# Weight conversion off GpSimd, even steps, and a shorter lag between front sequences, in an attention kernel followed by a low-rank mixer

## The chip, the cores and the metric

The kernel runs on one core of one Trainium2 chip. The metric is device time in microseconds (us). Runs of different sets were on different chips, so every kernel has runs of the kernel before beside it on its own chip, and ratios are taken only within such a set.

## The reference

Linear attention with decay, over blocks of 64, then a mixer of low rank over the sequence and a two-layer network. In short (4 batches, 8 heads, 768 positions, head width 64; rank 32; 512 channels; 2048 hidden):

```python
# attention, for each block of 64 positions and each head
intra = ((qb @ kb.T) * Dmask) @ vb
inter = (qb * lam_pow) @ kv_state
kv_state = lam_block * kv_state + (kb * rev_pow).T @ vb
# ... heads side by side give x: (4, 768, 512)
h = xt @ U @ V                      # over the sequence, rank 32
u = x + h.T
out = u + np.maximum(u @ w_ch1, 0.0) @ w_ch2
```

U, V, w_ch1 and w_ch2 are float64. The kernel reads them as pairs of 32-bit words and makes float32 of them itself; this is the "conversion" below.

## The kernel before

It has three stages: a **front** (attention, mix, and the transposes that the network needs), the **hidden** layer (`u @ w_ch1`, results stored to memory), and the **second product**. Each float32 product is done as three matmuls of rounded parts, which is why `u` and the weights exist as high part, low part and difference.

The conversion of one tile of 128x512, in steps that are called one at a time between other work:

```python
def one():
    hi = st["w"][:, :, 1]
    ...
    nc.vector.tensor_scalar(sc, hi, 20, 0x7FF, ALU.logical_shift_right, ALU.bitwise_and)      # L110
    nc.gpsimd.tensor_scalar(sc_f, sc, 1151.0, 896.0, ALU.min, ALU.max)                        # L111
    nc.gpsimd.tensor_scalar(sc, sc_f, -896.0, float(1 << 23), ALU.add, ALU.mult)              # L112
    nc.vector.tensor_scalar(m, hi, 0xFFFFF, 0x100000, ALU.bitwise_and, ALU.bitwise_or)        # L113

def two():
    ...
    nc.vector.scalar_tensor_tensor(m_f, lo, 2.0**-32, m, ALU.mult, ALU.add)                   # L121
    nc.vector.scalar_tensor_tensor(sc, hi, 0x80000000, sc, ALU.bitwise_and, ALU.bitwise_or)   # L122
    nc.vector.scalar_tensor_tensor(dst(), m_f, 2.0**-20, sc_f, ALU.mult, ALU.mult)            # L123

def three():                                   # the three parts of a weight tile
    nc.vector.tensor_scalar(t.bitcast(U32), w.bitcast(U32), HI, None, ALU.bitwise_and)        # L139
    nc.scalar.copy(o[:, 0, :], t)
    nc.gpsimd.tensor_tensor(out=low, in0=w, in1=t, op=ALU.subtract)                           # L141
    nc.scalar.mul(o[:, 1, :], low, 4096.0)
    nc.vector.scalar_tensor_tensor(o[:, 2, :], t, -E, low, ALU.mult, ALU.add)                 # L143
```

The front is four batches, each a list of 38 small "pieces" (transpose q and k, scores, outputs, transpose back; then two pieces `low` and `low_sum` for the mixer, then mix and turn). Batches 0 and 2 form sequence one, batches 1 and 3 sequence two, of 76 pieces each; the two are interleaved with a lag, and after every second piece one conversion step is called:

```python
one = front(0) + front(2)
two = front(1) + front(3)
lag = 3 * NT                                   # 18 pieces
merged = one[:lag]
for i in range(lag, len(one)):
    merged += [one[i], two[i - lag]]
merged += two[len(one) - lag :]
...
side = U's steps + v_steps(0) + v_steps(1) + w1_steps(0) + w1_steps(1)    # (shortened)
for i, (what, s) in enumerate(merged):
    run[what](s)
    if side and i % 2 == 1:
        side.pop(0)()
```

## Time and profile before

The time was 754.97 us, the median of 3 runs (751.0 to 755.06). The stages of the profiled run, of span 752.2 us, are read from the first and last matmul of each:

| stage | us |
|---|---|
| front, to the first hidden matmul | 198.0 |
| hidden layer | 279.5 |
| second product | 270.1 |
| end | 4.7 |

The groups of VectorE's conversion instructions, with shapes kept apart: busy time and mean of one in ns, then idle time before them.

```profile
L113 DVE TENSOR_SCALAR m<-words 128x512 uint32<-128x512 uint32 x32 | 31.5, 983 | 0.0
L121 DVE SCALAR_TENSOR_TENSOR m<-words,m 128x512 f32<-128x512 uint32 x32 | 30.1, 941 | 0.9
L139 DVE TENSOR_SCALAR wt<-wf 128x512 uint32<-128x512 uint32 x32 | 13.6, 426 | 1.7
```

L113 and L139 are the same kind of work at the same size, yet L113 takes over twice as long: GpSimd has often just begun its own work when L113 comes. By the timelines, 16 of the 32 took 1.49 to 1.52 us, each begun 0.1 us after GpSimd's subtract L141; of the others, 15 took 0.41 to 0.47.

Second, the chain of work that ended last, for the front (start, length, what):

```profile
24.07 10.12 DMA words<-in_moe_V_dram
...
41.78 8.75 DMA words<-in_moe_V_dram
```

Third, windows over the front up to the first `low` (its copy on ScalarE starts at 68.17 us) and from the first to the last `low` (184.63 us). The columns are the stretch, its length, then busy time and count of TensorE's matmuls, its weight loads, VectorE, ScalarE and GpSimd, then granted clock, share of DMA and GB/s:

```profile
8.00:68.17 60.17, 46.85 (x519) 40.32 (x520) 35.64 (x80) 18.03 (x33) 12.75 (x16) 0.86 0.63 146
68.17:184.63 116.46, 107.48 (x1315) 85.65 (x1313) 94.51 (x203) 52.31 (x95) 18.99 (x19) 1.00 0.56 145
```

### The profile page before, as it was taken

The numbers are of one execution on the slowest core, as the hardware profiler recorded it, in microseconds if no ns is written. First come the engines' busy times: TensorE is split into PE (matmuls) and PEld (weight loads), VectorE is DVE, ScalarE is ACT, GpSimd is POOL, SyncE is SP. The second block draws the span as 40 slices with busy tenths as digits, with TensorE's granted clock in tenths as the row PEclk, the third lists the DMA queues.
The fourth block names the chain that finished last, engine by engine and source line by source line (L and its number), as shares of the span: only waits on it lengthen the run. The fifth ranks groups of instructions, "written<-read, shape, count | busy, mean of one in ns | idle before, by whom it ended". The sixth has DMA issues, their size and how long they took to land.

```text
span 752.2 us, 11331 instructions
## 1 busy us (share of the span) xinstructions
PE 711.0 (95%) x4176; PEld 566.5 (75%) x4176; DVE 549.2 (73%) x961; ACT 234.6 (31%) x409; POOL 150.3 (20%) x150
## 2 busy tenths in 40 slices
PE   6669899997999999999999999999999999999997
PEld 5567668785668866888888888788888888888885
DVE  4567878795998988877677753567767676676764
ACT  2334444443223233232333322223223232322320
POOL 1213211110014444433333320002003030020300
PEclk9978999999799999999999999999999999999999
DMA  6664766750326657665565479995536335363531
GB/s 158 155 148 115 196 168 168 169 142 16 112 93 247 199 196 263 212 217 183 191 223 215 169 261 364 313 347 182 184 97 197 102 136 168 94 201 98 155 98 56
DMA packets 131808, 131.77 MB, mean 175 GB/s; under 512 B 81320, under 2 KB 89512, under 8 KB 131752
## 3 DMA queue, kind: packets, MB, share of 16 engines
q1 hardware_dynamic: 131752, 131.04, 55.1%
q8 instruction: 33, 0.54, 0.3%
q14 instruction: 23, 0.19, 0.1%
HBM read 80.68 MB, written 50.33 MB: 174 GB/s over the span
## 4 chain that ended last, share of the span: by engine, by line
PE 74%; DVE 14%; issue 4%; DMA 3%; POOL 3%; ACT 1%; SPq 1%; DVEq 0%; POOLq 0%; ACTq 0%
PE pz L512 17%; PE pz L607 12%; PE pz L606 12%; PE pd L608 12%; PE pd L518 9%; DMA words<-in_moe_V_dram 3%; PE px L302 2%; PE ps L280 2%; PE px L297 2%; DVE kv L328 2%; DVE r L526 1%; DVE sm L285 1%; DVE sc L122 1%; DVE ut L395 1%; DVE w L143 1%
## 5 line engine op out<-in xcount | busy, mean ns | idle before, releaser
L512 PE MATMUL pz<-u_hl,w 128*128 128x512 f32 x768 | 190.6, 398 | 1.9 <-ACT r L525 1.9
L512 PEld LDWEIGHTS pz<-u_hl,w 128*128 128x128 f32 x768 | 144.6, 189 | 38.9 <-ACT r L525 4.4
L608 PE MATMUL pd<-w_d,m 128*128 128x512 f32 x384 | 152.3, 397 | 0.0
L607 PE MATMUL pz<-w_hl,m 128*128 128x512 f32 x384 | 152.2, 396 | 0.0
L606 PE MATMUL pz<-w_hl,m 128*128 128x512 f32 x384 | 152.2, 396 | 0.0
L591 ACT ACTIVATE m<-mt 128x512 fp32r<-128x512 f32 x96 | 60.6, 632 | 192.6 <-PE pd L608 138.0
L592 DVE SCALAR_TENSOR_TENSOR m<-rm,m 128x512 fp32r<-128x512 f32 x96 | 71.4, 745 | 51.0 <-ACT m L591 50.6
L518 PE MATMUL pd<-u_d,w 128*128 128x512 f32 x384 | 100.7, 399 | 3.6 <-DVE u_d L501 2.7
L518 PEld LDWEIGHTS pd<-u_d,w 128*128 128x128 f32 x384 | 71.7, 188 | 24.4 <-DVE u_d L501 3.7
L608 PEld LDWEIGHTS pd<-w_d,m 128*128 128x128 f32 x384 | 72.3, 188 | 18.0 <-DVE r L526 0.4
L607 PEld LDWEIGHTS pz<-w_hl,m 128*128 128x128 f32 x384 | 72.3, 188 | 17.6
L606 PEld LDWEIGHTS pz<-w_hl,m 128*128 128x128 f32 x384 | 72.3, 188 | 17.6
L526 DVE SCALAR_TENSOR_TENSOR r<-pd,r 128x512 f32<-128x512 f32 x96 | 61.6, 682 | 32.1 <-ACT r L525 31.1
L628 POOL TENSOR_TENSOR o<-o,u 128x512 f32<-128x512 f32 x20 | 29.7, 1522 | 237.9 <-DVE o L626 237.9
L141 POOL TENSOR_TENSOR wl<-wf,wt 128x512 f32<-128x512 f32 x32 | 42.2, 1317 | 151.4 <-DVE wt L139 101.0
L593 DVE SCALAR_TENSOR_TENSOR m<-m 128x512 fp32r<-128x512 f32 x96 | 69.0, 720 | 0.9
L525 ACT ACTIVATE r<-pz 128x512 f32<-128x512 f32 x96 | 51.7, 592 | 56.2 <-PE pz L512 56.2
L590 DVE TENSOR_SCALAR mt<-rm 128x512 uint32<-128x512 uint32 x96 | 46.2, 481 | 29.4 <-DMA rm<-r_d 28.7
L140 ACT CAST w<-wt 128x512 fp32r<-128x512 f32 x32 | 19.9, 622 | 101.1 <-issue 63.6
L302 PE MATMUL px<-sm,vraw 128*64 128x128 f32 x384 | 40.4, 296 | 6.8 <-DVE sm L285 5.6
L261 POOL TENSOR_TENSOR ks<-kraw,rev 128x512 f32<-128x512 f32 x20 | 21.5, 1074 | 101.9 <-PE pkv L318 63.9
L297 PE MATMUL px<-qs,kv 128*64 128x128 f32 x320 | 35.9, 289 | 4.9 <-DVE kv L328 4.9
(70 smaller groups left out, 785.3 us busy)
## 6 DMA issues: line engine op xcount, KB each, us to landing
r_d<-r SPq DMA_DIRECT2D x96, 256.0 KB, 3.1
rm<-r_d SPq DMA_DIRECT2D x96, 256.0 KB, 2.7
words<-in_moe_w_ch_dram SPq DMA_DIRECT2D x32, 512.0 KB, 4.0
w_d<-w SPq DMA_DIRECT2D x16, 768.0 KB, 3.3
w_hl<-w_d SPq DMA_DIRECT2D x16, 512.0 KB, 6.0
qraw<-in_q_dram SPq DMA_DIRECT2D x24, 256.0 KB, 3.9
kraw<-in_k_dram SPq DMA_DIRECT2D x24, 256.0 KB, 3.7
vraw<-in_v_dram SPq DMA_DIRECT2D x24, 256.0 KB, 3.7
```

The costliest lines, as they stand in the source:

```text
L297: nc.tensor.matmul(out=px[rows, a, :], lhsT=kvs[b % 2][:, a, rows], rhs=qs[:, a, :], start=True, stop=False,)
L302: nc.tensor.matmul(out=px[x * D : (x + 1) * D, a, :], lhsT=vr[:, 2 * a + x, :], rhs=sm[:, x, a, :], start=(c == 0), stop=True,)
L512: nc.tensor.matmul(out=acc[g][0], lhsT=w[:, n, ct, :], rhs=uhl[g][:, n, ct, :], start=(ct == 0 and n == 0), stop=(ct == CT - 1 and n == 1),)
L518: nc.tensor.matmul(out=acc[g][1], lhsT=w[:, 2, ct, :], rhs=ud[g][:, ct, :], start=(ct == 0), stop=(ct == CT - 1),)
L525: nc.scalar.mul(r, pz, 1.0 + E)
L526: nc.vector.scalar_tensor_tensor(r, pd, 4096.0, r, ALU.mult, ALU.add)
L591: nc.scalar.activation(out=m[:, 0], in_=t, func=AF.Relu)
L592: nc.vector.scalar_tensor_tensor(m[:, 1], r, 0.0, hi, ALU.max, ALU.subtract)
L593: nc.vector.scalar_tensor_tensor(m[:, 2], hi, E, low, ALU.mult, ALU.subtract)
L606: nc.tensor.matmul(out=pz, lhsT=m[:, 0, cols], rhs=hl[:, 0], start=first, stop=False)
L607: nc.tensor.matmul(out=pz, lhsT=m[:, 1, cols], rhs=hl[:, 1], start=False, stop=end)
L608: nc.tensor.matmul(out=pd, lhsT=m[:, 2, cols], rhs=dd, start=first, stop=end)
```

## The change

Its intent: take GpSimd out of the conversion, so that it no longer slows VectorE (983 ns for L113 against 426 for L139) nor keeps it waiting (19.9 us ahead of L143, 8.7 ahead of L122); let the first two w1 tiles share the hidden units in which `u`'s differences are made, so that VectorE isn't full there; and start the second sequence sooner. Stores of `u` move one step later and q and k get a third buffer.

```diff
+    def set_ends(t):
+        nc.vector.memset(t[:, 0:1], 1151.0)
+        nc.vector.memset(t[:, 1:2], 255.0 * (1 << 23))
 ...
-            nc.gpsimd.tensor_scalar(sc_f, sc, 1151.0, 896.0, ALU.min, ALU.max)
-            nc.gpsimd.tensor_scalar(sc, sc_f, -896.0, float(1 << 23), ALU.add, ALU.mult)
             nc.vector.tensor_scalar(m, hi, 0xFFFFF, 0x100000, ...)
+            nc.scalar.activation(out=sc_f, in_=sc, func=AF.Relu, bias=ends[-1][:, 0:1], scale=-1.0)
+            nc.scalar.activation(out=sc, in_=sc_f, func=AF.Relu, bias=ends[-1][:, 1:2], scale=-float(1 << 23))
 ...
-            nc.gpsimd.tensor_tensor(out=low, in0=w, in1=t, op=ALU.subtract)
+            nc.vector.tensor_tensor(out=low, in0=w, in1=t, op=ALU.subtract)
 ... load():
-            ... bufs=4 if name == "v" else 2
+            ... bufs=4 if name == "v" else 3
 ... (zeros, rev, lamh now share one tile `small`; `pt` takes a turn in the ring of temporaries)
 ... mix():
-        nc.sync.dma_start(out=u_d[s], in_=xs[s])
 ... turn():
-        del xs[s]
+        nc.sync.dma_start(out=u_d[s], in_=xs.pop(s))
 ...
-    lag = 3 * NT
+    lag = 2 * NT
 ...
-    side += w1_steps(0) + w1_steps(1)
+    late = w1_steps(0) + w1_steps(1)
 ...
         if side and i % 2 == 1:
             side.pop(0)()
+        elif late and i > 4 * NT and i % 7 == 0:
+            late.pop(0)()
 ... hidden layer:
-    for ft in range(LAST):
-        side = w1_steps(ft + 2) + w2_steps(ft)
-        for i, pair in enumerate(pairs):
+    head = [(pair, ft) for pair in pairs for ft in (0, 1)]
+    body = [(pair, ft) for ft in range(2, LAST) for pair in pairs]
+    tail = [(pair, ft) for pair in pairs for ft in range(LAST, FT)]
 ... (the steps of a stretch are spread evenly over all of its units)
```

More of the change, by code (lines that the diff above doesn't have):

```diff
@@ L72 @@
     words_pool = [wconv]
+    ends = []
+    def set_ends(t):
+        nc.vector.memset(t[:, 0:1], 1151.0)
+        nc.vector.memset(t[:, 1:2], 255.0 * (1 << 23))
+        ends.append(t)
     u_d = [dram.tile([P, C], FP32, name=f"u_d{s}") for s in range(NS)]
@@ L110, in one @@
             nc.vector.tensor_scalar(sc, hi, 20, 0x7FF, ALU.logical_shift_right, ALU.bitwise_and)
-            nc.gpsimd.tensor_scalar(sc_f, sc, 1151.0, 896.0, ALU.min, ALU.max)
-            nc.gpsimd.tensor_scalar(sc, sc_f, -896.0, float(1 << 23), ALU.add, ALU.mult)
             nc.vector.tensor_scalar(m, hi, 0xFFFFF, 0x100000, ALU.bitwise_and, ALU.bitwise_or)
+            nc.scalar.activation(out=sc_f, in_=sc, func=AF.Relu, bias=ends[-1][:, 0:1], scale=-1.0)
+            nc.scalar.activation(
+                out=sc, in_=sc_f, func=AF.Relu, bias=ends[-1][:, 1:2], scale=-float(1 << 23)
+            )
         def two():
@@ L179, in load @@
         t = raw_pool.tile(
-            [P, H, D], FP32, tag=f"{name}raw", bufs=4 if name == "v" else 2, name=f"{name}raw"
+            [P, H, D], FP32, tag=f"{name}raw", bufs=4 if name == "v" else 3, name=f"{name}raw"
         )
@@ L193 @@
     v_hl, p_hl = vp[:, 0:S], vp[:, S : S + C]
+    set_ends(vp[:, S + C : S + C + 2].bitcast(FP32))
     ident = consts.tile([P, P], FP32, name="ident")
     gather = consts.tile([P, G, R], FP32, name="gather")
-    zeros = consts.tile([P, 1], FP32, name="zeros")
+    small = consts.tile([P, 16], FP32, name="small")
+    zeros = small[:, 0:1]
     mask = consts.tile([P, 2, HP, P], FP32, name="mask")
-    rev = consts.tile([P, 2, HP], FP32, name="rev")
-    lamh = consts.tile([P, HP], FP32, name="lamh")
+    rev = small[:, 8:16].rearrange("p (x a) -> p x a", x=2)
+    lamh = small[:, 4:8]
     powq = consts.tile([P, HP, P], FP32, name="powq")
@@ L355, in low @@
             )
-        pts[b] = att.tile([P, C], FP32, tag="pt", bufs=1, name="pt")
+        pts[b] = tmp("pt")
         nc.scalar.copy(pts[b], pp)
@@ L474 @@
             side.pop(0)()
-    for step in side:
+        elif late and i > 4 * NT and i % 7 == 0:
+            late.pop(0)()
+    for step in side + late:
         step()
@@ L490 @@
     )
+    set_ends(r_pool.tile([P, 2], FP32, tag="ends", bufs=1, name="ends"))
     def banks():
@@ L551, with run_units @@
     LAST = FT - 3
-    for ft in range(LAST):
-        side = w1_steps(ft + 2) + w2_steps(ft)
-        for i, pair in enumerate(pairs):
+    head = [(pair, ft) for pair in pairs for ft in (0, 1)]
+    body = [(pair, ft) for ft in range(2, LAST) for pair in pairs]
+    tail = [(pair, ft) for pair in pairs for ft in range(LAST, FT)]
+    def run_units(units, side, every=lambda i: None):
+        for i, (pair, ft) in enumerate(units):
             if ft == 0:
@@ L558 @@
             hidden(ft, pair)
-            for step in side[len(side) * i // len(pairs) : len(side) * (i + 1) // len(pairs)]:
+            for step in side[len(side) * i // len(units) : len(side) * (i + 1) // len(units)]:
                 step()
-    units = [(pair, ft) for pair in pairs for ft in range(LAST, FT)]
+            every(i)
+    run_units(head, w1_steps(2))
+    side = []
+    for ft in range(3, FT - 1):
+        side += w1_steps(ft) + w2_steps(ft - 3)
+    side += w2_steps(FT - 4)
+    run_units(body, side)
     side = w1_steps(FT - 1)
@@ L565 @@
     backs = list(range(FT))
-    for i, (pair, ft) in enumerate(units[:6]):
-        hidden(ft, pair)
-        for step in side[len(side) * i // 6 : len(side) * (i + 1) // 6]:
-            step()
-        if i >= 2:
-            w2_back(backs.pop(0))
+    run_units(tail[:6], side, lambda i: w2_back(backs.pop(0)) if i >= 2 else None)
     mid_ctx.close()
@@ L637, in ahead @@
             split(i + 2)
-    for i, (pair, ft) in enumerate(units[6:]):
+    for i, (pair, ft) in enumerate(tail[6:]):
         hidden(ft, pair)
```

## The prediction

> **What bounds the kernel now.** I read the slices of the page first, then windows over the stages, then the waits, and last the timelines of single engines. The slices show where TensorE is not full:
>
> ```profile
> PE   6669899997999999999999999999999999999997
> DVE  4567878795998988877677753567767676676764
> PEclk9978999999799999999999999999999999999999
> ```
>
> A slice is 18.8 us. TensorE is short in slices 0 to 2 (0 to 56 us) and slice 9 (169 to 188 us); elsewhere it looks full, but a busy PE is a modelled one, so I counted matmuls. The first hidden-layer matmul (pz of the first w1 tile) starts at 197.96 us, the first of the second product at 477.4, and the last ends near 747.5. These windows give the pace (span, then busy time and count for PE, PEld, DVE, ACT, POOL):
>
> ```profile
> 197.00:285.00 88.00, 83.62 (x345) 63.98 (x345) 80.88 (x127) 26.83 (x49) 30.05 (x31) 0.99 0.52 179
> 300.00:440.00 140.00, 140.00 (x600) 112.53 (x599) 108.67 (x168) 46.53 (x85) 50.87 (x52) 1.00 0.58 205
> 440.00:477.40 37.40, 37.40 (x161) 30.10 (x160) 14.48 (x24) 10.03 (x18) 0.29 (x1) 1.00 0.92 324
> 477.40:747.50 270.10, 270.10 (x1153) 216.71 (x1152) 187.31 (x307) 69.70 (x113) 29.75 (x20) 1.00 0.49 159
> ```
>
> In the last row 1152 matmuls take 270.1 us, 0.2345 us each without a gap. The hidden layer has 1152 too and takes 279.5 us (197.9 to 477.4), so it loses 279.5 - 270.1 = 9.4 us. At 0.2345 us, the 88 us of the first row would hold 375 matmuls; there are 345, so 7 us are lost there, and the rest before 300 us. In that stretch VectorE is 92% busy; from 440 to 477 it is 39% busy. VectorE is the bound early and has slack late. The time is thus 198 (front: attention and mix) + 279.5 + 270 + 4.7 (end), and only the first two can move.
>
> Inside the hidden stretch, VectorE does the differences u_d first and is then made slow by GpSimd:
>
> ```profile
> 200.22 6.10 DVE L501 SCALAR_TENSOR_TENSOR u_d<-u_hl 128x512 fp32r<-128x512 f32 x10
> ...
> 284.67 1.34 POOL L141 TENSOR_TENSOR wl<-wf,wt 128x512 f32<-128x512 f32 x1 [2.00 <-DVE wt L139]
> 284.77 1.52 DVE L113 TENSOR_SCALAR m<-words 128x512 uint32<-128x512 uint32 x1
> ...
> 290.54 0.42 DVE L113 TENSOR_SCALAR m<-words 128x512 uint32<-128x512 uint32 x1
> ```
>
> The same TENSOR_SCALAR takes 0.42 us alone and 1.52 us when GpSimd's subtract began just before it. The waits add two more, and one in the DMA queue:
>
> ```profile
> DVE w L143 <- POOL wl L141: 19.9, 15, 1.5
> DVE sc L122 <- POOL sc L112: 9.1, 18, 0.5
> SPq L379 <- DVE x_nat L378: 45.2, 21, 16.0
> ```
>
> In the front the chain of waits gives a stretch that is bound by latency at either end. At the far end, with one sequence alone:
>
> ```profile
> 185.27 1.13 PE L361 MATMUL pr<-pt,gather 128*128 128x512 f32 x2 [0.71 <-ACT pt L357]
> 188.00 0.83 PE L375 MATMUL pu<-vp 128*128 128x512 f32 x2 [1.60 <-DVE vp L368]
> ```
>
> and near the start VectorE, in order, stands still for V's words:
>
> ```profile
> 50.55 0.36 DVE L110 TENSOR_SCALAR sc<-words 128x384 uint32<-128x384 uint32 x1 [6.35 <-DMA words<-in_moe_V_dram]
> ```
>
> [...] 0.42 us for L113 alone, 0.68 to 0.69 us for the two-input instructions; so the subtract that moves to VectorE costs about 0.69. [...] the trace has no such form, and its Relu of 128x512 without that bias is 0.63 us. One table load is in the trace, and Relu is already used, so I count no new one.
>
> **Part 1, conversion without GpSimd.** VectorE's cost of one w tile before, from the group rows (128x512 forms): L110 0.42, L113 0.98, L121 0.94, L122 0.69, L123 0.69, L139 0.43, L143 0.75: 4.90 us, plus waits for GpSimd (19.9 + 9.1) / 32 = 0.91: 5.81. After: L113 falls to 0.42, L121 to 0.69 and L143 to 0.69, the subtract adds 0.69, the waits fall to nearly nothing: 0.42 + 0.42 + 0.69 + 0.69 + 0.69 + 0.43 + 0.69 + 0.69 = 4.72. That is 1.1 us a tile, 35 us of VectorE over 32 tiles, and GpSimd's 96 conversion instructions (42 + 31 + 24 us) go. [...] Off the path after 300 us, on it before.
>
> **Part 2, u's differences over two tiles and even steps.** From 197 to 300 us VectorE has u_d 24 x 0.61 (spacing in the timeline) = 15, r 30 x 0.61 = 18, and 12 conversions x 5.81 = 70: together 103 us in 103. It is exactly full. After, the first six units (34 us of TensorE, 5.63 each) hold the 24 u_d, 12 r and one conversion: 15 + 7 + 5 = 27 us. Then each unit holds 2 r and 25 conversions / 33 units: 1.3 + 0.76 x 4.72 = 4.9 of 5.63 us, 87%. So no backlog builds. What stays is the first unit: its eight u_d (4.9 us) start only after the last turn, while pz covers 3.75 us; TensorE lost 0.95 us there by the page's wait, and the cold clock (0.57 between 190 and 200 us) adds some. I keep 3 us of the 9.4: gain 6.5.
>
> **Part 3, shorter lag.** Each sequence has 76 pieces. With lag 18 the merged list has 18 solo, 58 pairs, 18 solo; with lag 12 it has 12, 64, 12. From the PE timeline: the second sequence's first transposes come at 43.86 us, the last paired ones near 174.2. So the first solo stretch is 8 to 44 us (36 us), the pairs take 130 us (2.25 each), the last solo stretch 24 us. After: the first twelve pieces end at 28.6 us in this trace, 64 pairs at 2.25 make 144, and the last twelve, mixes and turns alone, run from 188 to 198 today: 10 us. The chain low, pt, low_sum, vp before them (182.7 to 188) now lies beside the other sequence's last turns; I leave 2 us of it exposed. Sum 28.6 + 144 + 2 + 10 = 184.6. The first V wait (3.75 us) falls inside the pairs and I add 3 for it: 187.6 against 198, gain 10.5. The w1 conversions, which filled VectorE from 62 to 82 us, are now thinned; I count that gain as paid by the pairs becoming heavier, since attention beside attention needs more TensorE per pair than attention beside mixing.
>
> **Part 4, stores later and a third q and k buffer.** The waits of the DMA queue on transposes and on GpSimd's ks (19.0 + 15.1 us) and on the mixes (45.2) shrink, but TensorE's own waits on q and k in the front are 8.3 + 0.6 us, most of that at the start, where nothing changes. I count 0 to 1 us.
>
> **Sum.** 755 - 6.5 - 10.5 - 0.5 = 737.5, rounded to 737.
>
> **Rivals.** First, ScalarE takes GpSimd's place: L122 waits for two ACTIVATEs in line behind evictions that wait for TensorE. For it: ScalarE works in order, and its evictions wait 56 us for pz. Against it: VectorE's own evictions wait for the same units, and steps lie apart. It would give back 3 to 6 us: 741 to 743. Second, the front is bound by VectorE's total (147 us busy of 200) or by the loads, not by the solo ends: then the pairs stretch to 2.4 us, eating 10 us, and the front stays near 197: about 747. For it: VectorE is 0.92 full from 60 to 140 in places (9.84 of 10 us in 90 to 100). Third, the opposite: with GpSimd out of the way and no queue held by a waiting store, pairs fall to 2.1 us: another 10 us, about 727.
>
> **Range and chances.** The hidden gain is firm within 2 us, being bounded by 9.4; the front is wide, from 0 to 20. That gives 725 to 749 for 8 in 10. A gain over 2% means below 739.9; my centre is only just past it, and improvement by the third rival is a bit likelier than the second: 0.62 faster, 0.35 within 2%, 0.03 slower.
>
> **What would show it.** Right: L113 at 0.42 us throughout; no idle TensorE between the third unit and 300 us; first pz near 187 us; hidden layer from first pz to second product 272 to 274 us; second product still 270. Wrong: first pz later than 195 us (part 3 fails); VectorE waiting for ScalarE before L122 for over 10 us in all (first rival); TensorE waiting for u_d in the second or third unit (part 2); or a V wait longer than 6 us that now stops both sequences.

The time of an ACTIVATE with a bias per partition did not come from a trace ("the trace has no such form" speaks of that ACTIVATE). With the 0.63 us of the trace, 70 such instructions are an estimated 44 us on the 234.6 of its page, 37% of the span of 752.2. "In order" can be seen in the same trace: VectorE stood until 34.21 us for V's words, and the mask product behind them ran at 36.75, though its scores were done at 29.8. For ScalarE the profile after shows it, below. The "cold clock" is the granted clock that the windows show: at 0.50, from 190 to 198 us, a matmul of the last turns (put) took a median 421 ns, where the median of 81 of them from 89.8 us on is 273.

## More of the kernel before

V's words come in two fetches, each of 32 rows broadcast to four groups of 32 partitions:

```python
moe_V[:, cols].unsqueeze(0).broadcast_to([G, R, SH])      # G = 4, R = 32, SH = 384
```

## The result, and the profile after

The changed kernel takes 745.02 us (median of 4, 744.11 to 745.43), the kernel before beside it 754.33 (751.0 to 755.06). Ratios here are the mean time of one kernel's runs over that of the kernel before in the same rounds, so not quite the ratio of the medians. Here it is 0.9883, with a 95% interval of 0.9852 to 0.9915: a gain of 1.2%, within 2%.

The time is inside the predicted range, but 8 us above its centre: about 9 us came of the 17.5 that the sum promised. By stages of the profiled runs:

| stage | before | after | gain predicted | gain measured |
|---|---|---|---|---|
| front | 198.0 | 196.3 | 10.5 (+0.5) | 1.7 |
| hidden | 279.5 | 272.0 | 6.5 | 7.5 |
| second product | 270.1 | 270.1 | 0 | 0 |

**The hidden layer did what was planned.** The slices of the page, first:

```profile
PE   5679999998799999999999999999999999999997
DVE  4677989569999996677777934578758676676764
ACT  2353535335225654544555522223222232322320
PEclk9899999999999999999999999999999999999999
```

TensorE is short in slices 0 to 2 as before; the notch that was in slice 9 now lies across slices 9 and 10 (8 and 7), and all after that is full but for the end. ScalarE is fuller than before in the front and in the hidden layer. TensorE's granted clock (the last row) is 0.9 or more from slice 2 on, so it is not what kept the front from gaining. The windows over the hidden layer and the second product say it exactly:

```profile
196.30:468.30 272.00, 270.55 (x1155) 216.77 (x1154) 206.28 (x367) 127.92 (x219) 0.00 (x0) 1.00 0.63 219
468.30:738.40 270.10, 270.08 (x1153) 216.79 (x1151) 187.35 (x308) 69.66 (x113) 29.80 (x20) 1.00 0.50 161
```

Of the 9.4 us that the hidden layer lost, under 2 are left, and GpSimd does nothing there. What is left is one wait, in the first unit, for `u`'s differences (the wait list of the stretch from 196 to 300 us: total, times, longest):

```profile
PE pd L533 <- DVE u_d L516: 1.5, 1, 1.5
```

The conversion's own instructions, in the form of the rows shown of before (L113 is now L118, L121 is L131, L122 is L132; the subtract is L151; L120 is the first of the two new ScalarE instructions):

```profile
L118 DVE TENSOR_SCALAR m<-words 128x512 uint32<-128x512 uint32 x32 | 13.4, 420 | 0.0
L131 DVE SCALAR_TENSOR_TENSOR m<-words,m 128x512 f32<-128x512 uint32 x32 | 22.0, 687 | 0.5
L132 DVE SCALAR_TENSOR_TENSOR sc<-words,sc 128x512 uint32<-128x512 uint32 x32 | 22.3, 696 | 0.5 <-ACT sc L121 0.5
L151 DVE TENSOR_TENSOR wl<-wf,wt 128x512 f32<-128x512 f32 x32 | 22.0, 687 | 1.1
L120 ACT ACTIVATE sc<-sc,ends 128x512 f32<-128x512 uint32 x30 | 21.8, 727 | 4.9 <-DVE sc L117 3.9
```

L118 fell from 983 to 420 ns and L131 from 941 to 687. VectorE's waits on ScalarE ahead of L132 come to 0.5 us over 32 tiles.

**The front did not.** The windows for the same two stretches, up to the first `low` (here at 73.50 us) and on to the last:

```profile
8.00:73.50 65.50, 51.81 (x646) 42.83 (x648) 41.43 (x99) 25.62 (x47) 9.73 (x9) 0.95 0.80 165
73.50:182.67 109.17, 103.28 (x1186) 80.20 (x1187) 89.42 (x186) 50.21 (x90) 11.65 (x11) 0.98 0.53 132
```

With the shorter lag the first `low` has 36 pieces ahead of it in program order instead of 30 (12 alone and 24 paired, against 18 alone and 12 paired). The first stretch grew by 5.3 us and the second shrank by 7.3; TensorE's time without a matmul in the first is 13.7 us, as it was (13.3), although the granted clock was higher there (0.95 against 0.86). Overlap moved work to an earlier stretch; it did not fill the holes.

The largest hole can be followed from engine to engine in the timelines. Columns: start, length, engine, line, what, and in brackets the idle time before it and what ended it. First VectorE, then ScalarE, about 33 us; then TensorE, with two later lines that mark the first `low` (pp) and the last `low_sum` (pr):

```profile
32.93 0.36 DVE L117 TENSOR_SCALAR sc<-words 128x384 uint32<-128x384 uint32 x1 [3.92 <-DMA words<-in_moe_V_dram]
...
34.50 1.22 DVE L297 TENSOR_TENSOR sm<-ps,mask 128x1024 f32<-128x1024 f32 x1
```

```profile
33.33 0.62 ACT L120 ACTIVATE sc<-sc,vp 128x384 f32<-128x384 uint32 x1 [5.70 <-DVE sc L117]
33.85 0.57 ACT L265 COPY qt<-pq 128x512 f32<-128x512 f32 x1
```

```profile
28.31 0.66 PE L260 MATMUL pq<-ident,qraw 128*128 128x128 f32 x4
...
35.87 2.08 PE L292 MATMUL ps<-qt,kt 64*128 64x128 f32 x16 [6.03 <-DVE sm L297]
...
71.52 1.91 PE L364 MATMUL pp<-x_nat,u_w 128*32 128x512 f32 x12
...
183.30 1.13 PE L373 MATMUL pr<-pt,gather 128*128 128x512 f32 x2 [0.18 <-ACT pt L369]
```

VectorE stands at L117 for V's words, 3.92 us, and the mask product L297, which frees the only scores bank, stands behind it: it ran at 34.50, though its scores (27.22, 1.16 us long) were done at 28.4. ScalarE now has a conversion instruction of V too, for which it stood 5.70 us, and the copy of q (33.85), whose transpose was made at 28.31, stands behind that. TensorE has nothing for 6.03 us. In the kernel before, ScalarE had no such instruction and made the copy of q that was due there at 30.95 us, while VectorE stood from 30.46 to 34.21. The chain shows the same two fetches as before, 9.60 us from 23.31 on and 8.77 from 36.22 on.

Which block do the transposes at 28.31 belong to? They are the fifth of the trace, and in program order the fifth are the second sequence's first. The rest of the trace agrees. The scores at 35.87 are made from them, and the second sequence's first outputs, known by their 16 matmuls without a state term, come at 47.76. Of the scores after the first sequence's fourth (27.22), only those at 35.87 are done by then. So the second sequence started at 28.3 us, where the prediction had put it (28.6), and this hole lies inside the pairs.

### The profile page after: what moved, and what is told of

Read it like the earlier page. It is cut to its first block, busy times and chain, and to the rows that moved or that the text cites. A ratio compares the mean times of both kernels' runs of the same rounds, so it can differ in the third digit from the quotient of the medians.

```text
span 743.2 us, 11311 instructions
## 1 busy us (share of the span) xinstructions
PE 706.7 (95%) x4176; PEld 562.9 (76%) x4176; DVE 542.1 (73%) x997; ACT 280.2 (38%) x479; POOL 52.8 (7%) x48
## 4 chain that ended last, share of the span: by engine, by line
PE 85%; DVE 7%; DMA 4%; ACT 2%; issue 1%; SPq 1%; DVEq 0%; ACTq 0%
PE pz L527 24%; PE pd L533 12%; PE pz L629 12%; PE pz L628 12%; PE pd L630 12%; DMA words<-in_moe_V_dram 2%; PE px L314 2%; PE px L309 2%; PE ps L292 2%; DVE sm L297 1%; PE pkv L330 1%; DVE kv L340 1%; PE pxn L352 1%; PE put L402 1%; PE pk L260 1%
## 5 line engine op out<-in xcount | busy, mean ns | idle before, releaser
L527 PE MATMUL pz<-u_hl,w 128*128 128x512 f32 x768 | 187.8, 397 | 0.0
L533 PE MATMUL pd<-u_d,w 128*128 128x512 f32 x384 | 98.3, 397 | 1.5 <-DVE u_d L516 1.5
L650 POOL TENSOR_TENSOR o<-o,u 128x512 f32<-128x512 f32 x20 | 29.8, 1522 | 501.7 <-DVE o L648 501.7
L292 PE MATMUL ps<-qt,kt 64*128 64x128 f32 x384 | 34.1, 301 | 7.6 <-DVE sm L297 6.9
L292 PEld LDWEIGHTS ps<-qt,kt 64*128 64x128 f32 x384 | 27.3, 198 | 15.4 <-ACT kt L266 7.3
L297 DVE TENSOR_TENSOR sm<-ps,mask 128x1024 f32<-128x1024 f32 x24 | 29.4, 1223 | 8.4 <-PE ps L292 8.0
```

What stands on the lines that cost most here:

```text
L292: nc.tensor.matmul(out=ps[:, x, a, :], lhsT=kt[rows, a, :], rhs=qt[rows, a, :], start=True, stop=True,)
L527: nc.tensor.matmul(out=acc[g][0], lhsT=w[:, n, ct, :], rhs=uhl[g][:, n, ct, :], start=(ct == 0 and n == 0), stop=(ct == CT - 1 and n == 1),)
L533: nc.tensor.matmul(out=acc[g][1], lhsT=w[:, 2, ct, :], rhs=ud[g][:, ct, :], start=(ct == 0), stop=(ct == CT - 1),)
```

## The experiments

Four theories were open. **Lag**: the front gained little because a shorter lag is worth little. **V's words**: the wait for them, with other work behind it on VectorE, sets the front. **Buffers or stores**: the third buffer or the late store takes something back. **Parts**: one part of the change does nearly all, and others take from it.

"After" is the changed kernel. The first four ran together (before beside them: 749.94 us, 7 runs); the next four together (751.43, 7 runs); the last four together, with more rounds (751.47, 11 runs). All results were correct except where said. "First pz" is the front's length in the profiled run. The kernel before and that of experiment 8 have the same source text in the front, and the first pz of their profiled runs is at 198.0 and 194.7; so differences of 2 to 3 us in one profiled front are not read.

**1. The lag back at 18, in the changed kernel.**

```diff
-    lag = 2 * NT
+    lag = 3 * NT
```

> The changed kernel with the old lag of 18 pieces. Theory T (the shorter lag brought next to nothing, because the second sequence starts at 39 us and not at 28.6: VectorE stands in line for V's words): 745 to 748 us, first hidden matmul at 196 to 199 us. The prediction's own view (the lag is worth 10 us and something else in the change took it back): 753 to 756 us.

Measured: 743.39 us, ratio 0.9901 (0.9865 to 0.9936); first pz 196.0. The changed kernel has 0.9883 and 196.3. The shorter lag, from which the prediction had its 10.5 us, is worth nothing that can be measured here.

**2. Two q and k buffers again, in the changed kernel.**

```diff
-... bufs=4 if name == "v" else 3
+... bufs=4 if name == "v" else 2
```

> The changed kernel with two buffers for q and k instead of three. Theory T: no effect beyond 1 us, 744 to 746. Rival (the third buffer lets q and k loads crowd out V's words, which land 9 us late): 740 to 743, with V's words landing sooner.

Measured: 745.92 us, ratio 0.9928 (0.9899 to 0.9956); first pz 198.1. Not better than with three.

**3. `u` stored at once again, in the changed kernel** (the store back in `mix`, `del xs[s]` back in `turn`).

> The changed kernel with u stored in the mix again. Theory T: 744 to 747, the order of the stores does not bind. Rival (x tiles come free later now, as the 3.76 and 1.88 us of u stores in the chain say): 740 to 743, and those two waits leave the chain.

Measured: 743.18 us, ratio 0.9894 (0.9864 to 0.9923); first pz 196.2. The place of the store does not matter.

**4. V's words fetched whole and early**, just after the first six loads, into a w1 tile that is free then; the conversion steps stay where they are.

```diff
+    vw = w1_pool.tile([P, 3, C], F32R, tag="w1", name="vw").rearrange("p n c -> p (n c)")
+    nc.sync.dma_start(out=vwords[0], in_=moe_V.bitcast(U32).unsqueeze(0).broadcast_to([G, R, 2 * S]))
```

> The changed kernel with V's words fetched whole right after the first six loads, into a w1 buffer that is free then; the conversion steps stay where they were. Theory T (VectorE's stand for V's words at 29 to 33 and 43 to 45 us is what ate the lag's gain): second sequence's first transposes near 30 us, first hidden matmul 187 to 190, total 736 to 739. Rival P (the pairs run at TensorE's and VectorE's own pace, so an earlier start is lost again in the middle): 743 to 746, although the waits are gone.

Measured: 747.96 us, ratio 0.9953 (0.9925 to 0.9982); first pz 199.8. VectorE's wait for V fell from 5.9 us to nothing, but its wait for U's words rose to 8.9, and the front got longer. The wait was moved rather than removed: U's words, behind the early fetch in the queue, went out at 23.71 us instead of 16.19. This neither helps nor refutes the theory of V's words.

**5. V's steps called later, in the changed kernel**, at pieces 7, 20, 22, 24, 25, 30, 32 and 34 instead of one at every second piece.

> The changed kernel with V's conversion steps moved from pieces 7 to 21 to pieces 7 to 34: fetched at the same place, used later. Theory V (the front's start is held by VectorE and now ScalarE too standing in line for V's words, 28.8 to 35.9 us): those waits vanish, first hidden matmul 5 to 9 us earlier (187 to 191 us), total 736 to 740. Theory L (the start is held by the loads of q, k and v): within 2 us of the changed kernel, 743 to 746.

Measured: 748.91 us (744.23 to 750.48), ratio 0.9955 (0.9911 to 0.9999); first pz 196.1 in the profile, which was the fastest of the four runs. VectorE's wait for V fell from 5.9 to 2.3 us and the front did not move: the twelve pairs up to the first `low` took 42.1 us (29.73 to 71.78), against 43.2 in the changed kernel (28.31 to 71.52). So in the kernel with the short lag, less standing for V is not a shorter front.

**6. q, k and v read as one run of 2 KB per partition** instead of eight of 256 bytes. This gives a wrong result on purpose (relative error 1.34): it asks only if the small runs of the loads slow the front.

```diff
-            out=t, in_=source[b, :, c * P : (c + 1) * P, :].rearrange("h p d -> p h d")
+            out=t, in_=source[b].rearrange("h s d -> (h s d)")[...].rearrange("(p h d) -> p h d", h=H, d=D),
```

> The changed kernel with q, k and v read as runs of 2 KB for each partition instead of eight of 256 bytes, the same bytes from other places, so the result is wrong on purpose. Theory L (loads hold the first 70 us): the low-rank product of the first sequence comes 10 us or more before 73.5 us and first hidden matmul is at 184 to 189 us, total 732 to 738. Theory V: V's words arrive somewhat sooner behind shorter queues, 2 to 4 us, total 740 to 743. Theory T2 (the middle runs at TensorE's pace whatever arrives when): the stretch from the first low-rank product to the last stays at 107 to 110 us in either case.

Measured: 747.25 us, ratio 0.9955 (0.9919 to 0.9992); first pz 195.5. The loads landed sooner (q a median 3.4 us after its issue, not 4.9) and the front did not move. But VectorE's waits for V rose to 10.5 us, which may hide a gain; V's words still took 8.2 us from issue to the instruction that stood for them (13.35 to 21.59 us).

**7. The conversion alone, in the kernel before**: only the edits of `one`, `three` and `set_ends`. Lag 18, two buffers, old order of the hidden units, w1's steps at their old place.

> The kernel before with the conversion on VectorE and ScalarE alone, nothing else. If taking GpSimd out alone clears the backlog: hidden layer (first pz to second product) 274 to 276 us instead of 279.5, total 3 to 6 us less. The one-place-in-line reading adds: ScalarE stands for V's words as well, front 0 to 3 us longer.

Measured: 738.69 us (736.24 to 742.34), ratio 0.9834 (0.9794 to 0.9873): the lowest ratio, though the interval reaches across 0.98, so that a gain of over 2% stays unclear. It was on another chip than the whole change (0.9883, 0.9852 to 0.9915), and the two intervals still touch; the kernels of the last set, which are this one with one addition each, bear it out below. In the profile (its fastest run) the first pz is at 187.9 and the hidden layer takes:

```profile
187.90:459.70 271.80, 271.30 (x1154) 217.22 (x1153) 206.97 (x370) 128.83 (x221) 0.00 (x0) 1.00 0.63 223
```

So the conversion alone has all of the hidden layer's gain, and gains in the front besides, with the lag as it was.

**8. The order of the hidden units alone, in the kernel before**: `head`, `body`, `tail` with even steps, conversion on GpSimd as it was.

> The kernel before with only the order of hidden-layer units changed (u's differences over two w1 tiles, steps spread evenly), GpSimd kept. If the backlog comes from u's differences: hidden layer 272 to 274 us, total 5 to 7 us less[...].

A branch is cut from it: 276 to 279 us if what GpSimd does to VectorE is the greater part.

Measured: 744.51 us, ratio 0.9913 (0.988 to 0.9946); first pz 194.7 (198.0 in the kernel before; nothing of the front's source is changed, so this shows how far apart two profiled fronts can lie). The hidden layer:

```profile
194.70:470.00 275.30, 273.09 (x1154) 216.99 (x1153) 216.81 (x336) 88.19 (x161) 86.77 (x88) 1.00 0.61 216
```

It gains 4.2 us, with GpSimd at work (275.3 lies between the two branches). Conversion alone gains 7.7, both together 7.5: the two remedies are for the same shortage, and once GpSimd is gone, the new order adds nothing.

**9. Conversion alone plus the lag of 12.**

```diff
-    lag = 3 * NT
+    lag = 2 * NT
```

> The conversion change alone (which ran in 738.7 us, first hidden matmul at 187.9) plus the lag of 12. If the shorter lag is what gives the front back: first hidden matmul at 193 to 197 us, total 743 to 746. If it is harmless or good: 184 to 189 us, 734 to 739.

Measured: 740.42 us, ratio 0.9852 (0.9823 to 0.9881); first pz 190.3. With experiment 1 this is the second pair in which the lag differs, and again there is no gain (0.9834 with 18). Its windows, to the first `low` at 71.77 us and on to the last:

```profile
8.00:71.77 63.77, 54.03 (x646) 45.16 (x648) 43.47 (x104) 27.91 (x51) 10.24 (x9) 0.92 0.67 159
71.77:177.30 105.53, 101.47 (x1185) 79.15 (x1186) 85.78 (x179) 46.57 (x85) 11.64 (x11) 1.00 0.54 142
```

The same two windows of conversion alone (first `low` at 60.39 us after 30 pieces, last at 174.61) are:

```profile
8.00:60.39 52.39, 41.69 (x522) 35.70 (x521) 37.06 (x81) 21.87 (x42) 7.42 (x7) 0.93 0.70 167
60.39:174.61 114.22, 107.25 (x1312) 85.75 (x1310) 93.89 (x203) 53.19 (x96) 13.95 (x13) 1.00 0.55 143
```

To the first `low`, counted from 8 us, a piece takes 52.39 / 30 = 1.75 us with lag 18 and 63.77 / 36 = 1.77 us with lag 12, though twice as many of them run in pairs. From there on it is 1.06 and 1.04 us per piece (108 and 101 pieces). In these two profiles the early pace does not depend on whether a piece has a partner.

**10. Conversion alone plus the third q and k buffer**, with `pt` in the ring of temporaries and the shared tile `small`, as the change has them.

> The conversion change alone plus the third q and k buffer (and the small tiles that make room for it), lag 18. If earlier q and k loads crowd the first transfers and V's words and that gives the front back: V's words land later than in the conversion alone (7.6 and 8.1 us), first hidden matmul 193 to 197 us, total 743 to 746. Otherwise 186 to 190 us, 737 to 740.

Measured: 747.64 us (744.08 to 751.68), ratio 0.9932 (0.9898 to 0.9966). The three other kernels of these rounds have conversion and one other addition and lie at 0.985 to 0.987, so this addition costs 0.7 to 0.8% more than those, about 6 us. The profiled run is the slowest of six, so its first pz of 203.2 is some 4 us too late to be typical. Its waits differ from those of conversion alone. The queue in which transfers are issued, first with the third buffer, then of conversion alone:

```profile
40.99 0.37 SPq L192 DMA_DIRECT2D vraw<-in_v_dram  x1
41.46 0.57 SPq L107 DMA_DIRECT2D words<-in_moe_V_dram  x1
```

```profile
33.53 0.57 SPq L107 DMA_DIRECT2D words<-in_moe_V_dram  x1
36.75 0.37 SPq L192 DMA_DIRECT2D vraw<-in_v_dram  x1
```

The second fetch of V's words stands behind a load of v that waits for a free buffer (the queue issued nothing from 36.51 to 40.99 us), and goes out 7.9 us later. The loads land later too: q a median 4.7 us after its issue (3.5 without), k 4.7 (3.6). VectorE's waits for V come to 9.3 us against 2.8. But the kernel before, with two buffers, has the same order (the load of v at 41.32, the fetch at 41.78) and 10.1 us of such waits. So the third buffer is not needed for that order, and what costs the 6 us is not shown.

**11. Conversion alone plus w1's late steps** (`elif late and i > 4 * NT and i % 7 == 0`).

> The conversion change alone plus the w1 steps thinned out over the front. VectorE has slack in the middle, so no effect is expected, 736 to 740 us; if it is what gives the front back, 743 to 746.

Measured: 740.46 us, ratio 0.9854 (0.9824 to 0.9883); first pz 194.2 in a profile that was among its slower runs (742.52). No gain over 0.9834, and no loss that the intervals would show.

**12. Conversion alone, with the words of U and V fetched from ScalarE's queue.**

```diff
-            nc.sync.dma_start(out=shape(words, s.shape[-1]), in_=s)
+            queue = nc.scalar if n < C else nc.sync
+            queue.dma_start(out=shape(words, s.shape[-1]), in_=s)
```

> A try at a better version: the conversion change alone, with U's and V's words fetched through ScalarE's DMA queue, so that they need not stand behind loads of q, k and v in the one queue. If V's words come late because of the queue: they land in 4 to 6 us instead of 8, first hidden matmul 182 to 186 us, total 731 to 736. If the transfer itself is slow: no gain, 736 to 741.

Measured: 741.66 us, ratio 0.9866 (0.984 to 0.9891); first pz 192.1. The first fetch goes out 15 us sooner than from the other queue (7.56 against 22.67), and is still slow. VectorE meets the step that needs it sooner too, and stands for it:

```profile
16.07 0.36 DVE L118 TENSOR_SCALAR sc<-words 128x384 uint32<-128x384 uint32 x1 [5.07 <-DMA words<-in_moe_V_dram]
```

The run has one use: from 22.4 to 23.9 us the second fetch is the only traffic at all, so the trace shows it by itself (queue, packets, MB, share of the 16 DMA engines):

```profile
q10 hardware_dynamic: 45, 0.14, 25.6%
```

The share of a quarter is as much as four of the 16 engines busy without a pause, and the fetch moved 92 GB/s. The 512 KB of a weight tile's words land a median 3.9 us after issue; V's 384 KB take 7.3 to 10.1 us from issue to the instruction that stands for them, wherever VectorE stood for them. At 92 GB/s, 384 KB need an estimated 4.3 us with nothing beside them; what the rest is, start-up or sharing the engines with q, k and v, no run separates. No run changed the shape of this fetch (four fetches of 32 rows would), so why it took up only a quarter of the engines is not shown.

## Why the prediction was right or wrong

**What bounds the kernel: right for the hidden layer.** The loss of 9.4 us against the second product's pace was real and VectorE was its cause: with VectorE's work made lighter, 279.5 us became 272.0, and the floor is 270.1. The range held because it left the front wide (0 to 20 us); the centre needed part 3, which failed.

**Part 1, conversion: the instruction times were right.** Summed over the rows of the profile after, one tile costs VectorE 4.72 us, the figure predicted. Without GpSimd L121 fell from 941 to 687 ns, which the prediction took as given: in the timelines before it took 0.98 to 1.10 us where GpSimd's L111 or L112 ran beside it, and 0.68 to 0.69 elsewhere. In the profile after, the conversion's TENSOR_SCALAR instructions of 128x512 took 0.420 to 0.439 us, its SCALAR_TENSOR_TENSOR 0.685 to 0.696 and the TENSOR_TENSOR, the subtract, 0.687. The new ACTIVATE with a bias took 0.727 us, where the Relu without one took 0.63 in the trace before. There is one table load, as before, of 1.28 us. ScalarE came to 280.2 us, 38% of the span.

**Part 1's effect on the front was mis-sized.** The prediction says of the thinner conversions in the front: "I count that gain as paid by the pairs becoming heavier". That set the term to zero. Conversion alone moved the first pz from 198.0 to 187.9 us in the profile of its fastest run. By the ratio it is less: 0.9834 of 751.43 is 12.5 us saved, of which the hidden layer has 7.7, so about 5 are left for the front. With one other addition the first pz was 190.3, 192.1 and 194.2. So the term is some 5 us, or up to 10 by the profile, and not zero. In the whole change it does not show (1.7 us in the front).

**Part 2: right, but not needed.** The hidden layer took 272.0 us, within the predicted 272 to 274, with one wait of 1.5 us in the first unit and none after. Conversion alone does the same (271.8). The prediction didn't ask what each of the two parts would do without the other.

**Part 3: the step that failed.** It is "64 pairs at 2.25 make 144", with 3 us added for the first V wait. Its four terms, measured in TensorE's timeline of the changed kernel (second sequence's first transposes at 28.31, the last `low_sum` done at 184.43, the first mix after it at 186.63, first pz at 196.32):

| term | counted, us | measured, us |
|---|---|---|
| twelve pieces alone | 28.6 | 28.3 |
| 64 pairs | 144 + 3 | 156.1 |
| exposed chain | 2 | 2.2 |
| last twelve pieces | 10 | 9.7 |
| first pz | 187.6 | 196.3 |

The whole miss lies in the pairs: 2.44 us each. The 2.25 was an average over 58 pairs of two sorts. In the trace before, the six pairs ahead of the first `low` (43.86 to 65.56) took 3.6 us each, and the 52 after it (to 175.21) 2.11. With the lag of 12, twelve pairs lie ahead of the first `low`. They took 3.6 us each as well (28.31 to 71.52), and the 52 after it 2.17 (to 184.43). So each of the six pairs that the shorter lag brought in cost 3.6 us and not 2.25, which is 8 of the 12 us by which the pairs exceed 144; the slower later pairs are 3 more. In the early stretch a pair takes nearly the time of two pieces alone (18 of them took 36 us before, 2.0 each), so pairing gains little there; experiments 7 and 9 show the same at nearly equal clock (0.93 and 0.92). V's words are at most a part of it: with V's steps late (experiment 5) the twelve early pairs still took 3.5 us each. The expectation of experiment 1 that "the second sequence starts at 39 us" misread the trace: the transposes at 37.88 us are of the first sequence's fifth block. Two pairs of kernels, with 0.9883 against 0.9901 and 0.9834 against 0.9852, show that the lag is worth nothing measurable (the runs of a pair were not in one set, so only their ratios can be compared).

**Part 4 had the wrong sign, at least in one setting.** "I count 0 to 1 us" of gain. The store has no effect (0.9894). The third buffer with its two companions costs about 6 us on top of the conversion; in the whole change, taking the buffer out gained nothing.

**The rivals.** ScalarE in the place of GpSimd did not happen where it was feared, before L132 (0.5 us). It did in the front, at V's words. The second rival came true in its number and its rate: "the pairs stretch to 2.4 us, eating 10 us, and the front stays near 197: about 747", against 2.44, 196.3 and 745 measured, and the sign "first pz later than 195 us (part 3 fails)" with it. Its reasons, VectorE's total or the loads, are not shown: in the twelve early pairs VectorE was busy for 28.3 of 43.2 us, and loads that landed sooner (experiment 6: q in 3.4 us, not 4.9) did not move the front, though there VectorE stood longer for V. The third did not come: the later pairs took 2.11 us before and 2.17 after.

**What stays open.** The whole change (0.9883, and 0.989 to 0.996 in versions of it) lies above conversion alone with or without one harmless addition (0.983 to 0.987). The third buffer's set would account for that, as it does when it is added to the conversion, but taking the buffers alone out of the whole change gained nothing (0.9928), so which of buffer, ring and shared tile it is, and what the combination does, is not settled. Nor is what sets the early pace of 1.75 us per piece: less standing for V goes with a shorter front in two kernels (conversion alone 2.8 us of waits and 187.9; the kernel before 10.1 and 198.0), but experiments 5 (2.3 and 196.1) and 6 (10.5 and 195.5) break that order.

## What to carry to other kernels

Before crediting a change with filling a stretch, count how much idle time of the bounding engine is in it; here the solo stretch was cut by 15 us (from 43.9 to 28.3), but the holes before the first `low` stayed (13.3 and 13.7 us), and the pairs took the time back. Before multiplying by an average rate, ask which stretches it was taken over and which one will have more of the work: 2.25 us per pair was a mean of 3.6 and 2.1, and all the new pairs were of the slow sort. When an instruction moves to another engine, look at what stands behind it there at its worst moment (here a copy of q that ran at 33.85 us, its transpose made at 28.31), not only at that engine's total. And run each part alone: two parts that cure the same shortage don't add, a part put in for safety can cost more than another gains, and the version to keep here is the conversion alone, at 738.7 us.
